# A fused attention and SiLU kernel: weight sums moved to GpSimd, one run of exponentials in chunk 2, row sums later in chunks 3 to 6

## The chip, the cores and the metric

The kernel runs on one core of a Trainium2 chip. The metric is the device time of one execution in microseconds. A profile is one such execution; its span is some 2 us shorter than the time.

## The reference, cut to what matters

```python
q_s = softmax(q, over head_dim)          # exp, row sum, divide
k_s = softmax(k, over sequence)
kv  = einsum('bhsd,bhse->bhde', k_s, v)
x   = einsum('bhsd,bhde->bhse', q_s, kv)     # 8 batches, 8 heads, 576 rows, 64
x   = x.transpose(0, 2, 1, 3).reshape(4608, 512)
h   = x @ w_in                           # 512 -> 2048
out = (h * sigmoid(h)) @ w_out           # 2048 -> 512
```

## The kernel before

The 4608 rows are worked in nine chunks, 0 to 8 (0 has 576 rows, 1 has 448, the others 512). While TensorE computes the two products of one chunk, the attention of the next batch is woven in: ScalarE takes the exponentials, VectorE the row sums (`qsum`), GpSimd the normalisation (`qnorm`) and v's cast (`vcast`, into the tile vaug), a DMA the transpose of q (`tr_dma`), TensorE the `kv` product and the product with q (`xt`), which gives the next chunk's input XT. The silu results are the tile GT; PSUM, in banks, holds what TensorE computes until another engine has read it.

From chunk 2 on both products are done with seven block products instead of eight, which needs sums of weight blocks (`vsum` for the input weights, tiles TX; `wsum` for the output weights, tiles TW) and of activations. An instruction list is built by hand: `plan(t, i, f)` puts f in front of unit i of chunk t, `ahead(t, n, f)` counts in a finer unit, `trail` puts work behind a unit. The order of the list is the order on every engine and on the DMA queue, and this is the whole of the tuning.

```python
def product1(t, g, k):                  # input product, group g of two blocks, block product k
    ...                                 # banks of PSUM: A for k = 1, 2; B for 6, 7, 4; C for 5, 3
    if k == 1:   ... new("s1") = o      # copy s, on VectorE for g = 1, else on ScalarE
    elif k == 6: add(new("u2"), s1)     # VectorE reads bank B; product 7 then adds to bank B
    elif k == 7: add(new("u3"), s1)
    elif k == 2: silu(o)
    else:        add(x, x); silu(x)     # 5, 4, 3
...
def after(t, k, o):                     # the same for the output product, trailing by one chunk
    if k == 1:
        nc.scalar.activation(out=new("s1"), in_=o, func=ACT.Copy, scale=1.0)   # "copy s" below
    elif k == 6:
        add(new("u2"), WP[t, "s1"])
    ...
ORDER = (1, 6, 2, 7, 5, 4, 3)
...
def plan_attn(b, plan, ex, qs, vs, tp, ks, ox, lq, lkv, eng=nc.gpsimd):
    for i in range(4):
        plan(ex[i], exp ...)                              # two of q, two of k
    for cc in range(2):
        plan(qs[cc], lambda cc=cc: (qsum(b, cc), qnorm(b, cc, nc.gpsimd)))
        plan(vs[cc], lambda cc=cc: vcast(b, cc, eng))
    ...
    plan(lq, lambda: load(b + 1, "qt", q))                # the next q
    plan(lkv, ...)                                        # the next k and v
    plan(tp, lambda: tr_dma(b, nc.sync))                  # transpose of q, issued from SyncE
    for cc in range(2):
        plan(ks[cc], lambda cc=cc: (kv(b, cc), kvcopy(b, cc)))
    for cc in range(2):
        plan(ox[cc], lambda cc=cc: xt(b, cc))             # reads the transposed q (qT)
```

The softmax here doesn't subtract the row's maximum and nothing guards it: scores larger than these inputs give would overflow.

## Time and profile before

| | before |
|---|---|
| time | 288.26 us, median of 4 runs (287.57 to 288.55) |
| span of the profile | 286.7 us |
| TensorE busy | 262.6 us (92%) |
| VectorE, ScalarE, GpSimd busy | 215.9, 174.0, 52.3 us |

TensorE is the bound on the whole, but not everywhere. Below I cut the span at the first matmul of the input product of each chunk, because that instruction is easy to find and the stages then add up. The first fence is the view of stretches: start and end in us, length, busy time of TensorE, its weight loads, VectorE, ScalarE and GpSimd with numbers of instructions, granted TensorE clock (the share of full speed at which TensorE was let run), DMA share and GB/s. The stretches are chunk 1, chunk 2 and two of the four steady chunks that have attention (3 to 6).

```profile
49.76:74.76 25.00, 22.55 (x189) 10.39 (x189) 20.41 (x37) 14.61 (x24) 6.43 (x4) 1.00 0.82 261
74.76:102.93 28.17, 22.66 (x206) 12.25 (x205) 19.95 (x38) 22.64 (x31) 6.85 (x4) 1.00 0.71 222
131.98:160.53 28.55, 27.04 (x301) 21.41 (x300) 23.96 (x46) 19.92 (x30) 6.39 (x4) 1.00 0.63 181
160.53:189.10 28.57, 27.06 (x302) 21.40 (x301) 23.98 (x46) 19.92 (x30) 6.39 (x4) 1.00 0.60 183
```

The reader is to see that chunk 2 has 5.5 us without TensorE work, chunk 1 2.4 us, a steady chunk 1.5 us. The view of waits (engine and line that waited, for whom, us in total, times, longest) says what these were:

```profile
PE hps L287 <- DVE u L301: 9.7, 12, 2.5
PE hps L287 <- ACT s L315: 1.4, 1, 1.4
PE ops L438 <- DVE GT L230: 1.3, 2, 1.1
PE hps L209 <- DVE GT L230: 0.6, 1, 0.6
```

L287 is the input product from chunk 2 on, L301 the VectorE sum that frees its bank. Of the 9.7 us some 3.3 lie in chunk 2 and 5.9 in the four steady chunks. There the timeline (start, length, engine, line, idle before in brackets) shows the order that the change is about:

```profile
137.88 0.68 DVE L313 TENSOR_SCALAR s<-hps 128x512 f32<-128x512 f32 x1
138.47 1.34 DVE L107 TENSOR_REDUCE zq<-eq 128x18 f32<-128x1152 bf16 x1
140.10 0.63 DVE L301 SCALAR_TENSOR_TENSOR u<-hps,s 128x512 f32<-128x512 f32 x1
140.65 1.34 DVE L107 TENSOR_REDUCE zq<-eq 128x18 f32<-128x1152 bf16 x1
140.78 0.60 PE L287 MATMUL hps<-XS,TX 128*128 128x256 bf16 x4 [1.26 <-DVE u L301]
142.57 0.62 ACT L401 ACTIVATE s<-ops 128x512 f32<-128x512 f32 x1
143.32 1.04 PE L379 MATMUL ops<-W,GT 128*128 128x256 bf16 x8
145.64 2.73 SPq L124 DMA_TRANSPOSE qT<-eq  x1
152.74 0.41 PE L189 MATMUL o<-qT,kvn 64*64 64x320 bf16 x8
```

The first row sum (L107) stands in front of the sum u, and TensorE waits 1.26 us for u. The transpose (L124) goes out 13.7 us after the chunk's first matmul (131.98), and its reader (L189) comes 7.1 us after that, so there is slack.

### The profile page before, as it was taken

How to read it: one execution, taken by the hardware profiler on the slowest of the kernel's cores; microseconds unless marked ns; L12 is line 12 of the kernel's file. 1: busy time of each engine (PE TensorE's matmuls, PEld its weight loads, DVE VectorE, ACT ScalarE, POOL GpSimd, SP SyncE). 2: the span in 40 equal slices, each digit the busy share in tenths (PEclk: the TensorE clock that was granted, in tenths of full speed). 3: DMA queues.
4: the chain of work that ended last, by engine and by line, in shares of the span. 5: the costliest groups of instructions: out<-in, count | busy, mean ns of one | idle time of the engine just before them, and what ended most of it. 6: DMA issues, size and time to landing. Idle time of an engine off the chain costs nothing.

```text
span 286.7 us, 6264 instructions
## 1 busy us (share of the span) xinstructions
PE 262.6 (92%) x2529; PEld 186.5 (65%) x2546; DVE 215.9 (75%) x422; ACT 174.0 (61%) x277; POOL 52.3 (18%) x44
## 2 busy tenths in 40 slices
PE   8789999988994988999799979997999999999993
PEld 3456664434343546876688668866876888688782
DVE  2957667897447999788978897889788769958841
ACT  5646663753799589566956695669564455454300
POOL 0541140026017004400440044004400000000000
PEclk9979999999999999999999999999999999999999
DMA  7999998985819940598069705961513011301324
GB/s 255 285 195 285 293 283 236 365 273 92 321 18 266 292 151 3 93 359 269 7 79 377 263 10 98 363 239 31 111 31 82 10 39 38 75 8 34 82 63 110
DMA packets 42381, 46.48 MB, mean 162 GB/s; under 512 B 18544, under 2 KB 29808, under 8 KB 42352
## 3 DMA queue, kind: packets, MB, share of 16 engines
q1 hardware_dynamic: 37312, 38.35, 45.1%
q0 software_dynamic: 5040, 7.73, 12.2%
q8 instruction: 20, 0.33, 0.5%
q14 instruction: 9, 0.07, 0.1%
HBM read 36.70 MB, written 9.44 MB: 161 GB/s over the span
## 4 chain that ended last, share of the span: by engine, by line
PE 60%; DVE 23%; ACT 6%; DMA 4%; issue 2%; POOL 1%; SPq 1%; DVEq 0%; POOLq 0%
PE ops L379 25%; PE hps L287 16%; PE hps L209 10%; PE ops L438 5%; DVE u L301 5%; DMA vt<-in_v_dram 3%; DVE zq L107 3%; DVE TW L355 2%; PE kvps L155 2%; PE o L189 2%; DVE SW L343 2%; DVE GT L230 2%; DVE u L396 1%; DVE SW L337 1%; ACT GT L309 1%
## 5 line engine op out<-in xcount | busy, mean ns | idle before, releaser
L209 PE MATMUL hps<-XT,W 128*128 128x512 bf16 (+3 forms) x313 | 63.6, 342 | 1.7 <-DVE GT L230 0.6
L113 POOL TENSOR_TENSOR eq<-eq,rzq 128x1152 bf16<-128x1152 bf16 x14 | 29.6, 2117 | 137.7 <-DVE rzq L108 125.5
L309 ACT ACTIVATE GT<-u 128x512 bf16<-128x512 f32 x40 | 25.2, 630 | 46.0 <-DVE u L301 46.0
L209 PEld LDWEIGHTS <-W 128*128 128x128 bf16 x320 | 31.4, 100 | 27.0 <-issue 4.0
L379 PEld LDWEIGHTS <-GT 128*128 128x128 bf16 x448 | 43.8, 98 | 7.7
L301 DVE SCALAR_TENSOR_TENSOR u<-hps,s 128x512 f32<-128x512 f32 x40 | 27.1, 678 | 22.0 <-ACT s L315 14.8
L287 PEld LDWEIGHTS <-TX 128*128 128x128 bf16 x320 | 30.3, 97 | 15.9 <-issue 11.7
L287 PE MATMUL hps<-XS,TX 128*128 128x256 bf16 x240 | 34.8, 273 | 5.0 <-DVE u L301 5.0
L379 PEld LDWEIGHTS <-SW 128*128 128x128 bf16 x336 | 32.8, 98 | 4.0 <-DVE SW L339 0.2
L230 DVE SCALAR_TENSOR_TENSOR GT<-sg,hps 128x320 bf16<-128x320 f32 (+3 forms) x64 | 23.9, 414 | 13.0 <-ACT sg L218 12.5
L438 PE MATMUL ops<-W,GT 128*128 128x512 bf16 x119 | 31.5, 380 | 1.8 <-DVE GT L230 1.3
L218 ACT ACTIVATE sg<-hps 128x320 f32<-128x320 f32 (+2 forms) x48 | 21.3, 456 | 18.6 <-PE hps L209 10.3
L379 PE MATMUL ops<-TW,SW 128*128 128x256 bf16 x224 | 28.8, 273 | 0.0
L379 PE MATMUL ops<-TW,GT 128*128 128x256 bf16 x224 | 28.7, 273 | 0.0
L379 PE MATMUL ops<-W,GT 128*128 128x256 bf16 x224 | 28.7, 273 | 0.0
L107 DVE TENSOR_REDUCE zq<-eq 128x18 f32<-128x1152 bf16 x16 | 21.5, 1344 | 9.2 <-ACT eq L93 9.2
L301 DVE SCALAR_TENSOR_TENSOR u<-hps,u 128x512 f32<-128x512 f32 x40 | 27.4, 685 | 1.0
L287 PEld LDWEIGHTS <-W 128*128 128x128 bf16 x240 | 22.5, 98 | 7.5 <-issue 4.5
L287 PE MATMUL hps<-XT,W 128*128 128x256 bf16 x160 | 24.1, 273 | 1.4 <-ACT s L315 1.4
L200 ACT CAST XT<-o 128x512 bf16<-128x512 f32 (+3 forms) x36 | 18.3, 561 | 4.5 <-PE o L189 4.5
L438 PEld LDWEIGHTS <-GT 128*128 128x128 bf16 x128 | 12.3, 98 | 13.3 <-DVE GT L230 2.3
L234 ACT ACTIVATE GT<-hps 128x512 bf16<-128x512 f32 x32 | 17.5, 595 | 3.5 <-PE hps L209 3.2
(68 smaller groups left out, 337.1 us busy)
## 6 DMA issues: line engine op xcount, KB each, us to landing
qt<-in_q_dram SPq DMA_DIRECT2D x6, 1152.0 KB, 6.2
kt<-in_k_dram SPq DMA_DIRECT2D x6, 1152.0 KB, 7.4
vt<-in_v_dram SPq DMA_DIRECT2D x6, 1152.0 KB, 9.9
W<-in_moe_w_in_dram POOLq DMA_DIRECT2D x4, 512.0 KB, 9.7
W<-in_moe_w_out_dram POOLq DMA_DIRECT2D x4, 512.0 KB, 17.4
out_dram<-oq SPq DMA_DIRECT2D x16, 128.0 KB, 6.8
out_dram<-u SPq DMA_DIRECT2D x30, 64.0 KB, 2.1
out_dram<-u SPq DMA_DIRECT2D x13, 128.0 KB, 2.4
```

The costliest lines, as they stand in the source:

```text
L107: nc.vector.reduce_sum(out=st[b]["zq"][:, cc], in_=e, axis=AX.X)
L113: eng.tensor_tensor(out=e, in0=e, in1=r[:, :, :, None].to_broadcast([128, J, 2, D]), op=ALU.mult)
L200: nc.scalar.copy(out=x, in_=o1[g][:, 0:size])
L209: nc.tensor.matmul(out=hps[:, 0:size], lhsT=W1[:, c, fb * 128:(fb + 1) * 128], rhs=XT[t][:, c, off:off + size], start=(c == 0), stop=(c == ...
L218: nc.scalar.activation(out=sg[:, 0:size], in_=hps[:, 0:size], func=ACT.Tanh, scale=0.5)
L230: nc.vector.scalar_tensor_tensor(out=y, in0=sg[:, h], scalar=1.0, in1=hps[:, h], op0=ALU.add, op1=ALU.mult)
L234: nc.scalar.activation(out=y, in_=hps[:, h], func=ACT.Silu)
L287: nc.tensor.matmul(out=o[:, f, :], lhsT=l(c, 2 * g + f), rhs=r(c), start=bool(first and f == 0 and c == 0), stop=(c == HK - 1), skip_group ...
L301: nc.vector.scalar_tensor_tensor(out=out, in0=o, scalar=1.0, in1=x, op0=ALU.mult, op1=ALU.add)
L309: nc.scalar.activation(out=y, in_=x, func=ACT.Silu)
L379: nc.tensor.matmul(out=o[:, a, :], lhsT=l(f), rhs=r(f), start=bool(first and a == 0 and f == 0), stop=(f == HF - 1), skip_group_check=True,)
L438: nc.tensor.matmul(out=OP[t, tb], lhsT=GT[t][:, fc, tb * 128:(tb + 1) * 128], rhs=W2[:, fc, :], start=(fc == 0), stop=(fc == NFB - 1),)
```

## The change

The intent: take sixteen-bit weight sums off VectorE, which is busy for 20 of 25 us in chunk 1; give chunk 2 one run of exponentials and so two table loads fewer (in this trace ScalarE loads a table, for 1.28 us, each time that it goes from silu to exponentials or back), and interleave its two groups so that each group's VectorE work hides behind the other's matmuls; and put the row sums of the steady chunks behind the sums that TensorE waits for. A copy of one element on GpSimd (`gate`) keeps its sums behind VectorE's last input-weight sum. The line `y1` also brings the output product of chunk 1, and with it its stores, forward in chunk 2. The whole diff:

```diff
@@ xlist
-        p = sorted((7 * g + POS[m], g, m) for g in range(first, HF // 2) for m in ORDER)
+        if t == STD:
+            p = [(m, g, m) for m in ORDER for g in range(first, HF // 2)]
+        else:
+            p = sorted((7 * g + POS[m], g, m) for g in range(first, HF // 2) for m in ORDER)
@@
-    y1 = [(1, x) for x in (5, 6, 8, 9, 10, 11, 13, 14, 15)] + [(2, x) for x in (1, 3, 5, 7, 10, 13, 16)]
+    y1 = [(1, x) for x in (5, 6, 8, 9, 10, 11, 13, 14, 15)] + [(2, x) for x in (0, 1, 2, 3, 4, 6, 8)]
@@
     V = nc.vector
+    G = nc.gpsimd
     for i in range(4):
-        plan(1, i, lambda i=i: vsum(i, 4, HF))
-        plan(1, 4 + i, lambda i=i: wsum(i // 2, i % 2, V))
-        plan(2, 2 * i + 10, lambda i=i: wsum(2 + i // 2, i % 2, V))
-        plan(2, 2 * i + 4, lambda i=i: vsum(i, F0, 4))
+        ahead(1, (-3, -1, 1, 2)[i], lambda i=i: vsum(i, F0, HF))
+    plan(1, 3, lambda: G.tensor_copy(gate[:, 1:2], TX[3][0:1, 0, 0:1]))
+    for i in range(8):
+        plan(1, 3 if i < 4 else 12, lambda i=i: wsum(i // 2, i % 2, G))
@@
-    plan_attn(3, lambda i, f: plan(2, i, f), (4, 4, 9, 9), (6, 8), (9, 11), 10, (14, 16), (18, 20), 7, 12)
+    plan_attn(3, lambda i, f: plan(2, i, f), (2, 2, 2, 2), (4, 6), (6, 7), 8, (12, 15), (18, 20), 7, 10)
     for b in range(4, B):
-        plan_attn(b, lambda i, f: plan(b - 1, i, f), (1, 1, 1, 1), (5, 7), (6, 7), 10, (13, 16), (19, 21), 11, 12)
+        plan_attn(b, lambda i, f: plan(b - 1, i, f), (1, 1, 1, 1), (8, 10), (6, 9), 11, (13, 16), (20, 22), 11, 12)
```

## The prediction

> **What bounds the kernel now.** TensorE is busy 262.6 of 286.7 us (page, part 1); only its gaps can be won. By stretches and waits: the stage of chunk 1 (50-75 us) has 1.9 us of TensorE waits for VectorE's GT, chunk 2 (75-103 us) 5 us (2.5 us on a VectorE sum, 1.4 us on ScalarE's copy, behind five table loads of 1.28 us), and each of the four steady chunks with attention (103-218 us, 28.56 us apart) 1.5 us on VectorE's u, behind the row sum (1.34 us + 0.27 us).
>
> **Removed, added, moved.**
> VectorE loses eight output-weight sums (8.1 us with lock waits) and gains about 0 on the input-weight sums: four of 1536 columns, some 0.97 us each (from 0.39 at 512 and 0.68 at 1024), for 5.4 us in eight. Two table loads go: 2.6 us of ScalarE.
> GpSimd gains eight sums. It needs 2.12 us for 1152 columns of the same operation, so I estimate 1.9 us each, 15 us in all. The Trainium skill (GPSIMD Engine Reference, Engine selection) says GpSimd is about 2x slower with two inputs; this trace has 2.12 against VectorE's 1.36 us.
> The Trainium skill (SBUF — State Buffer, two separate sides) says that two-input VectorE work waits out a GpSimd instruction: the trace agrees, a sum at 59.6 us took 2.40 us instead of 0.68, ending as GpSimd's ended. Here the gate keeps the input sums out of it.
>
> **Chunk 1: 0 (-0.5 to +1).** VectorE's stalls vanish, but four GpSimd sums (55.1 to about 62.8) stand before the two q normalisations, so these end near 67.1, as now (66.9). v's cast and the transpose follow; TensorE meets the cast at 68 as now. The 1.9 us gained come back as a wait for GpSimd.
>
> **Chunk 2: -4 us (-5 to -2.5).** One exponential run; pairs of groups hide the VectorE latency; VectorE loses some 6 us. Some 1.6 us remain where the PSUM ring fills during the run, perhaps 1 us at the output of the transpose, which now sits behind six stores.
>
> **Chunks 3-6: +1.4 us each (-0.1 to +2).** The row sum's wait of 1.3 us disappears, but TensorE then meets its next limit: the second product's first half must wait for ScalarE's copy s, which ends 143.19 in the chunk starting at 132 (exponentials, table load, three silus before it). That product starts at 143.32 now. So nothing is gained. Meanwhile the row sum now stands behind a VectorE sum that waits for that same copy: first sum about 138.5 -> 143.8, second 140.65 -> 146.7, transpose 145.6 -> 150.8. The transpose lands 4.7 us after issue: 155.5. The unit that reads qT now comes near 154.0: a new wait of about 1.5 us. Its slack in the kernel before was 2.4 us (150.35 against 152.74).
>
> **Sum.** 288.4 + 0.1 - 4.0 + 4 x 1.4 = about 290. Predicted 289.9 us, 8 in 10 within 284.0 to 293.0. Chances: faster by over 2% 0.05, within 2% 0.87, slower 0.08.
>
> **What would show it.** Chunk 3's start 4 us earlier; steady spacing near 30 us instead of 28.56; TensorE waits at the qT matmuls (XT outputs) for a DMA, none on VectorE's u after the row sum; GpSimd sums of 1.9 us; in chunk 1 a TensorE wait for GpSimd's vaug near 66-68 us; three table loads in chunk 2's stretch instead of five.
>
> **What would make it wrong.** If the transpose lands sooner or ScalarE reaches copy s earlier, the steady chunks are neutral and the total is about 284.5. If GpSimd sums take longer than 2.1 us, chunk 1 grows. If VectorE's later row sums also stall second-group products, steady chunks cost more.

## The result, and the profile after

| | before | after |
|---|---|---|
| time, median of 4 runs | 288.26 us (287.57 to 288.55) | 300.26 us (298.92 to 300.85) |
| ratio | | 1.0413 (95%: 1.0371 to 1.0455) |
| span of the profile | 286.7 us | 298.7 us |
| VectorE, ScalarE, GpSimd busy | 215.9, 174.0, 52.3 us | 211.0, 172.0, 69.7 us |
| chunk 1 | 25.00 us | 27.09 us |
| chunk 2 | 28.17 us | 30.55 us |
| chunks 3 to 6 | 114.73 us | 122.91 us |
| from chunk 7's first matmul to the end | 69.0 us | 69.0 us |

The four stages account for the whole loss: 2.1 + 2.4 + 8.2 us, less 0.6 us by which chunk 1 began earlier in this profile (runs with identical code up to there differ by as much: it began at 48.4 to 49.8 us in the kernel before and in runs r2 and r6 below). VectorE, ScalarE and the number of table loads all went down as intended, and the kernel became slower.

The same view of stretches after the change: chunk 1, chunk 2, and chunks 4 and 5.

```profile
49.13:76.22 27.09, 23.97 (x192) 10.98 (x188) 15.88 (x31) 14.31 (x24) 22.05 (x13) 0.94 0.80 264
76.22:106.77 30.55, 23.47 (x208) 12.88 (x205) 14.79 (x31) 20.38 (x30) 7.55 (x5) 0.89 0.62 154
138.18:168.34 30.16, 27.67 (x303) 21.60 (x300) 24.89 (x46) 20.04 (x30) 6.44 (x4) 1.00 0.53 155
168.34:199.52 31.18, 27.67 (x303) 21.58 (x300) 24.95 (x46) 20.16 (x30) 6.69 (x4) 1.00 0.66 185
```

The column before the last two is new evidence: the granted clock was 0.94 and 0.89 in the two stages where it had been 1.00. The waits:

```profile
PE o L189 <- DMA qT<-eq: 9.3, 5, 5.5
PE hps L287 <- ACT s L315: 2.9, 4, 0.7
PE kvps L155 <- POOL vaug L100: 2.8, 1, 2.8
PE ops L379 <- ACT s L401: 2.1, 4, 0.5
PE hps L287 <- DVE s L313: 1.9, 4, 0.5
PE hps L287 <- DVE u L301: 1.4, 5, 0.6
```

TensorE's waits on VectorE's u fell from 9.7 to 1.4 us, as intended. In their place stands a wait that the kernel before did not have at all, on the transposed q (first line): 5.5 us of it in chunk 2. A second new one, 2.8 us on v's cast by GpSimd, is in chunk 1. The GpSimd timeline of chunk 1 and TensorE's instruction that waited:

```profile
54.31 4.20 POOL L355 TENSOR_TENSOR TW<-W 128x1024 bf16<-128x1024 bf16 x2
58.48 4.21 POOL L355 TENSOR_TENSOR TW<-W,TW 128x1024 bf16<-128x1024 bf16 x2
62.65 4.18 POOL L113 TENSOR_TENSOR eq<-eq,rzq 128x1152 bf16<-128x1152 bf16 x2
66.79 2.24 POOL L100 CAST vaug<-vt 128x1152 bf16<-128x1152 f32 x2
67.99 0.48 PE L155 MATMUL kvps<-vaug,ek 64*64 64x65 bf16 x36 [2.76 <-POOL vaug L100]
```

Chunk 2, the DMA queue of SyncE, first before the change:

```profile
84.01 0.37 SPq L84 DMA_DIRECT2D qt<-in_q_dram  x1
87.87 1.12 SPq L457 DMA_DIRECT2D out_dram<-oq  x2
89.10 2.83 SPq L124 DMA_TRANSPOSE qT<-eq  x1
```

and after it, with the wait behind it:

```profile
88.74 3.69 SPq L457 DMA_DIRECT2D out_dram<-oq  x6
92.48 0.58 SPq L84 DMA_DIRECT2D qt<-in_q_dram  x1
93.17 5.93 SPq L124 DMA_TRANSPOSE qT<-eq  x1
102.56 0.48 PE L189 MATMUL o<-qT,kvn 64*64 64x320 bf16 x4 [5.51 <-DMA qT<-eq]
```

The transpose stands behind six stores and directly behind a load of 1.15 MB; its issue took 5.93 us instead of 2.7, and it landed 9.3 us after the issue began, where 4.7 was the median before. Last, the steady chunk that answers to the one shown before (chunk 4, which here begins at 138.18):

```profile
145.07 0.68 DVE L313 TENSOR_SCALAR s<-hps 128x512 f32<-128x512 f32 x1
145.85 0.69 DVE L301 SCALAR_TENSOR_TENSOR u<-hps,s 128x512 f32<-128x512 f32 x1
148.78 0.62 ACT L401 ACTIVATE s<-ops 128x512 f32<-128x512 f32 x1
149.43 0.69 DVE L396 SCALAR_TENSOR_TENSOR u<-ops,s 128x512 f32<-128x512 f32 x1 [1.51 <-ACT s L401]
149.45 1.03 PE L379 MATMUL ops<-W,GT 128*128 128x256 bf16 x8 [0.51 <-ACT s L401]
150.04 1.34 DVE L107 TENSOR_REDUCE zq<-eq 128x18 f32<-128x1152 bf16 x1
154.09 0.60 PE L287 MATMUL hps<-XT,W 128*128 128x256 bf16 x4 [0.73 <-ACT s L315]
157.20 2.70 SPq L124 DMA_TRANSPOSE qT<-eq  x1
161.99 0.28 PE L189 MATMUL o<-qT,kvn 64*64 64x192 bf16 x4 [0.42 <-DMA qT<-eq]
```

The sum u now comes right behind the copy of L313, but TensorE meets ScalarE's copy s (L401) instead: its output product (L379) starts 11.27 us into the chunk, against 11.34 before (143.32 less 131.98). So nothing was won there. The first row sum starts 11.9 us into the chunk instead of 6.5, the transpose goes out 19.0 us into it instead of 13.7, and the second group's product waits for ScalarE (L315) behind late VectorE sums.

The new line for batches 4 to 7 does one thing more. The first cast of v (unit 6) now stands ahead of the normalisation (unit 8) in GpSimd's list, so it runs 2.6 to 4.5 us into each of these chunks (in the kernel before 10.4 to 10.9, behind the normalisation), and one two-input VectorE sum beside it takes 1.4 us instead of 0.4. TensorE's wait of up to 0.5 us for L313 (1.9 us in all four) follows. This is not what the chunks lose: in chunk 3 of run r3 below the cast comes later and the long sum is missing, and the chunk takes 31.37 us against 31.41 in the changed kernel.

### The profile page after: what moved, and what is told of

Read it like the earlier page. It is cut to its first block, busy times and chain, and to the rows that moved or that the text cites. A ratio compares the mean times of both kernels' runs of the same rounds, so it can differ in the third digit from the quotient of the medians.

```text
span 298.7 us, 6269 instructions
## 1 busy us (share of the span) xinstructions
PE 265.3 (89%) x2546; PEld 187.6 (63%) x2546; DVE 211.0 (71%) x410; ACT 172.0 (58%) x275; POOL 69.7 (23%) x53
## 4 chain that ended last, share of the span: by engine, by line
PE 33%; DMA 19%; ACT 15%; DVE 13%; POOL 8%; issue 6%; SPq 3%; POOLq 1%; DVEq 0%; ACTq 0%
PE ops L379 15%; PE hps L287 8%; DMA W<-in_moe_w_out_dram 7%; DMA qT<-eq 7%; PE hps L209 5%; POOL eq L113 4%; PE ops L438 4%; DVE zq L107 4%; ACT ek L93 4%; ACT eq L93 3%; DVE u L301 3%; DMA kt<-in_k_dram 2%; ACT GT L234 2%; ACT L234 2%; DVE u L396 2%
## 5 line engine op out<-in xcount | busy, mean ns | idle before, releaser
L379 PEld LDWEIGHTS <-GT 128*128 128x128 bf16 x448 | 43.8, 98 | 10.4 <-issue 2.8
L301 DVE SCALAR_TENSOR_TENSOR u<-hps,s 128x512 f32<-128x512 f32 x40 | 27.2, 683 | 18.5 <-PE hps L287 8.2
L379 PEld LDWEIGHTS <-SW 128*128 128x128 bf16 x336 | 32.8, 98 | 4.0 <-DVE SW L339 0.2
L287 PE MATMUL hps<-XS,TX 128*128 128x256 bf16 x240 | 34.6, 273 | 0.8 <-DVE u L301 0.8
L287 PEld LDWEIGHTS <-TX 128*128 128x128 bf16 x320 | 30.7, 99 | 7.0 <-issue 3.0
L438 PE MATMUL ops<-W,GT 128*128 128x512 bf16 x128 | 33.7, 387 | 1.1 <-DMA W<-in_moe_w_out_dram 0.9
L218 ACT ACTIVATE sg<-hps 128x320 f32<-128x320 f32 (+2 forms) x48 | 21.3, 454 | 20.2 <-PE hps L209 14.9
L379 PE MATMUL ops<-W,GT 128*128 128x256 bf16 x224 | 28.7, 272 | 2.1 <-ACT s L401 2.1
L287 PEld LDWEIGHTS <-W 128*128 128x128 bf16 x240 | 23.1, 99 | 11.6 <-issue 8.0
L100 POOL CAST vaug<-vt 128x1152 bf16<-128x1152 f32 x12 | 14.6, 1224 | 65.7 <-DMA vt<-in_v_dram 50.3
L379 PE MATMUL ops<-TW,SW 128*128 128x256 bf16 x224 | 28.8, 273 | 0.0
L379 PE MATMUL ops<-TW,GT 128*128 128x256 bf16 x224 | 28.7, 273 | 0.0
L287 PE MATMUL hps<-XT,W 128*128 128x256 bf16 x160 | 23.9, 273 | 4.8 <-ACT s L315 2.9
```

Source lines behind the costliest of these rows:

```text
L218: nc.scalar.activation(out=sg[:, 0:size], in_=hps[:, 0:size], func=ACT.Tanh, scale=0.5)
L287: nc.tensor.matmul(out=o[:, f, :], lhsT=l(c, 2 * g + f), rhs=r(c), start=bool(first and f == 0 and c == 0), stop=(c == HK - 1), skip_group ...
L301: nc.vector.scalar_tensor_tensor(out=out, in0=o, scalar=1.0, in1=x, op0=ALU.mult, op1=ALU.add)
L379: nc.tensor.matmul(out=o[:, a, :], lhsT=l(f), rhs=r(f), start=bool(first and a == 0 and f == 0), stop=(f == HF - 1), skip_group_check=True,)
L438: nc.tensor.matmul(out=OP[t, tb], lhsT=GT[t][:, fc, tb * 128:(tb + 1) * 128], rhs=W2[:, fc, :], start=(fc == 0), stop=(fc == NFB - 1),)
```

## The experiments

Twelve kernels ran; all were correct. Stage lengths are cut as above. "Changed kernel" is the kernel after. The theories that the expectations name are these. Theory 1: the steady chunks lose because the row sums stand behind a sum that waits for ScalarE's copy s. Theory 2: chunk 2 loses by the company and place of the transpose in the DMA queue. Theory 3: chunk 1 loses by GpSimd sums in front of the normalisation. Theory 4: a long wait also costs clock. Theory 5: in the kernel before, the wait for u is in the shadow of another limit.

### The row sums of chunks 3 to 6

**r1_rows_back**, the line for batches 4 to 7 put back:

```diff
-  (1, 1, 1, 1), (8, 10), (6, 9), 11, (13, 16), (20, 22), 11, 12)
+  (1, 1, 1, 1), (5, 7), (6, 7), 10, (13, 16), (19, 21), 11, 12)
```

> The changed kernel with only the placement of the row sums, casts, transpose and output units of batches 4 to 7 put back. Theory 1 (the four steady chunks cost 8.2 us because the row sum stands behind a sum that waits for ScalarE's copy s, so that the transpose is 5 us later): steady spacing back to 28.56 us, no TensorE wait for qT there, span about 290.5 us. Rival (the steady chunks are slow because they inherit VectorE or DMA lateness from chunk 2): spacing stays 30 to 31 us and the span stays near 298 us.

Measured: chunks 4 to 6 took 28.55 us each, no wait for qT was left in chunks 3 to 6, the span was 290.5 us. The rival fell: nothing is inherited from chunk 2.

**r2_rows_only**, the same line of the change put into the kernel before:

> The kernel before with only that placement of batches 4 to 7 taken from the change. Theory 1: chunks 0 to 2 as before (chunk 3 starts near 103 us), steady spacing 30 to 31.4 us, span about 295 us. Rival (the loss needs the rest of the change): spacing 28.6 us and a span near 287 us.

Measured: chunks 1 and 2 as before (24.99 and 28.18 us), chunks 3 to 6 123.16 us in sum against 114.73, span 293.9 us. The loss of the steady chunks needs nothing of the rest of the change.

**r12_only_sums_back**: of that line only the row sums (with the normalisations that follow them) put back.

```diff
-  (1, 1, 1, 1), (8, 10), (6, 9), 11, (13, 16), (20, 22), 11, 12)
+  (1, 1, 1, 1), (5, 7), (6, 9), 11, (13, 16), (20, 22), 11, 12)
```

> The changed kernel with only the row sums and normalisations of batches 4 to 7 put back to their two units; casts, transpose and output units stay where the change put them. If the place of the row sums is what costs the steady chunks: the transpose goes out 14 us after a chunk's first matmul as in the kernel before (19 in the changed one), no wait for qT in chunks 3 to 6, the wait of 1.3 us for u is back, spacing 28.4 to 28.7 us, span about 290.5. Rival (the later transpose, output units or cast cost it too): spacing over 29.2 us.

Measured: chunks 4 to 6 took 28.56 to 28.57 us; the transpose went out 14.0 us into chunk 4; the wait of 1.3 us for u was back and none for qT in these chunks; span 291.1 us. So it is the place of the row sums, not the units given to the casts, the transpose or its readers. (The first cast comes 10 to 11 us into the chunk again, behind the normalisation, though its unit is the change's.)

**r9_copy_dve**: is it ScalarE's copy s that makes them late, as theory 1 has it?

```diff
-        if k == 1:
+        if k == 1 and 2 <= t <= 5:
+            nc.vector.tensor_scalar_mul(out=new("s1"), in0=o, scalar1=1.0)
+        elif k == 1:
             nc.scalar.activation(out=new("s1"), in_=o, func=ACT.Copy, scale=1.0)
```

> The changed kernel with the copy s of the output product taken from ScalarE to VectorE in chunks 3 to 6 only (one more VectorE instruction of 0.68 us a chunk, one less on ScalarE). Theory 1 says that the row sums are late because the VectorE sum in front of them waits for ScalarE's copy behind the exponentials: then the first row sum starts 2 to 3 us earlier in the chunk, the transpose goes out about 2.5 us earlier (16.5 us after the chunk's first matmul instead of 19), no TensorE wait for qT over 0.3 us is left, nor one for copy s, and the spacing falls from 30.2 to 31.4 us to between 27.5 and 28.8. Rival (the sheer place of the row sums among VectorE's work makes them late, whoever copies s): the transpose moves by under 1 us and the spacing stays over 29.8 us.

Measured: the row sum of chunk 4 came 11.1 us into the chunk instead of 11.9, the transpose 18.3 instead of 19.0, and the chunk took 29.39 us instead of 30.16; the four took 119.6 us instead of 122.9. A wait for qT was left (8.9 us in all five chunks, 5.4 of it in chunk 2), and TensorE now waited up to 1.1 us for VectorE's own copy (L313), which stands behind the added one. The spacing lies between theory and rival. The 0.8 us is what is left of the copy's share after two things that this edit puts in front of the row sum: the added copy itself (0.7 us), and the sum held up beside the cast, which in the changed kernel is hidden behind the wait for copy s (1.51 us, shown above) and here is not. In chunk 3 of r11, which has the same later row sums and copy but no such hold-up, the row sum comes 10.0 us into the chunk, against 12.0 in chunk 3 of the changed kernel and 7.0 before. So ScalarE's copy is some 0.8 to 1.9 us net of the delay of about 5 us, and theory 1 holds in part: the rest is the place in VectorE's list, behind a sum that needs matmuls which only end 10 us into the chunk.

**r6_rows_sooner**: the kernel before with the first row sum one unit later only.

```diff
-  (1, 1, 1, 1), (5, 7), (6, 7), 10, (13, 16), (19, 21), 11, 12)
+  (1, 1, 1, 1), (6, 7), (6, 7), 10, (13, 16), (19, 21), 11, 12)
```

> The kernel before with the first row sum of batches 4 to 7 issued one unit later only, that is just behind the first product's sum u that TensorE waits 1.3 us for, and ahead of the sum that needs copy s. Theory 5 (that wait is in the shadow of ScalarE's copy s, behind the exponentials, so taking it away gains nothing): the wait for u falls from 1.3 us to under 0.3 us a chunk, a wait for copy s of about 1.4 us appears in its place, the spacing stays 28.5 us (within 0.15) and the span 286 to 287.5. Rival (the wait was worth its length, and the change only moved the row sums too far): spacing 27.2 us and a span near 281.

Measured: spacing 28.76 us (0.2 us longer than before, just outside what I had expected), span 287.0. The rival fell. But the wait did not pass to copy s as I had expected: both row sums now stand together in front of the next sum, and TensorE waits 1.8 us for that one. The run shows that the wait for u cannot be had back by this step; it doesn't show by itself that copy s is the limit.

### Chunk 2 and the transpose

**r3_load_behind**: in the line of batch 3, the load of the next q behind the transpose.

```diff
-  (2, 2, 2, 2), (4, 6), (6, 7), 8, (12, 15), (18, 20), 7, 10)
+  (2, 2, 2, 2), (4, 6), (6, 7), 8, (12, 15), (18, 20), 9, 10)
```

> The changed kernel with one line moved in chunk 2: the load of the next q (1.15 MB) is issued behind the transpose of batch 3 instead of just ahead of it. Theory 2 (the transpose landed 9.3 us after issue instead of 4.7 because it shares the DMA engines with that load): the transpose is still issued near 92.5 us, lands in 4.7 us near 97.3, TensorE's wait for qT in chunk 2 falls from 5.5 to about 0.5 us, and chunk 3 starts 5 to 6 us earlier. Rival (the transpose is only late because it stands behind six stores in the queue): landing stays 9 us and the wait stays over 4 us.

Measured: the transpose was issued at 91.11 us, in 2.82 us, and TensorE's wait ended at 97.48, 6.4 us after the issue instead of 9.4; the wait fell from 5.5 to 1.9 us and chunk 2 from 30.55 to 26.72 us. The company of the load is most of it. Some of the wait stays, more than expected, because the transpose still took 6.3 us to land and not 4.7.

**r7_tr_early**: also the transpose in front of the last four stores of chunk 1.

```diff
-  (2, 2, 2, 2), (4, 6), (6, 7), 8, (12, 15), (18, 20), 7, 10)
+  (2, 2, 2, 2), (4, 6), (6, 7), 6, (12, 15), (18, 20), 9, 10)
```

> The changed kernel with, in chunk 2, the transpose of batch 3 issued ahead of the last four of the eight output stores of chunk 1, and the load of the next q behind it. Theory 2 (place in the queue and company of the load together make the 5.5 us wait): the transpose goes out near 90 us, as soon as its input is normalised, TensorE's wait for qT in chunk 2 is under 0.7 us, chunk 2 lasts 25 to 26 us instead of 30.5, 2 to 3 us less than in the kernel before. Rival (something else holds chunk 2 back, as the PSUM ring or the exponentials): it stays above 27 us.

Measured: the transpose landed 4.8 us after its issue, there was no wait for qT in chunk 2, and the chunk took 24.53 us, 3.6 us less than in the kernel before. The queue of SyncE, to be held against the one shown above:

```profile
88.38 2.41 SPq L457 DMA_DIRECT2D out_dram<-oq  x4
90.89 2.81 SPq L124 DMA_TRANSPOSE qT<-eq  x1
93.80 2.48 SPq L457 DMA_DIRECT2D out_dram<-oq  x4
96.33 1.05 SPq L84 DMA_DIRECT2D qt<-in_q_dram  x1
```

The Trainium skill (DMA: Bandwidth & Descriptors, Queues, rings and completion order) says that one issuing engine's descriptors are consumed in ring order on each DMA engine. The three runs agree with it: the transpose landed 9.3 us after its issue with the load in front of it (changed kernel), and 6.3 and 4.8 us with the load behind it (r3 and r7). A run with the place alone mended, the load still in front, was not made.

### Chunk 1 and GpSimd

**r4_sums_late**: the GpSimd sums behind the normalisations.

```diff
-        plan(1, 3 if i < 4 else 12, lambda i=i: wsum(i // 2, i % 2, G))
+        plan(1, 12, ...wsum(i // 2, i % 2, G)) if i < 4 else plan(2, 9, ...wsum(i // 2, i % 2, G))
```

> The changed kernel with the eight GpSimd sums moved behind the q normalisations: four behind v's casts in chunk 1, four in chunk 2. Theory 3 (in chunk 1 TensorE waits 2.8 us for v's cast because four GpSimd sums of 2.1 us stand in front of it, and the granted clock of 0.62 in the 4 us after that wait costs another 1.5 us): no wait for vaug, granted clock 1.00 between 64 and 72 us, chunk 2 starts near 72 us instead of 76.2. Rival (what delays the cast is the late row sums on VectorE, not GpSimd's own work): the wait stays at 2 us or more.

Measured: no wait for v's cast, granted clock 1.00 from 60 to 76 us, chunk 1 22.71 us: 4.4 less than in the changed kernel and 2.3 less than before. Chunk 2 began at 71.4 us. In the GpSimd timeline the normalisations now come as soon as the row sums are there:

```profile
57.30 2.12 POOL L113 TENSOR_TENSOR eq<-eq,rzq 128x1152 bf16<-128x1152 bf16 x1 [3.37 <-ACT sg L218]
59.87 2.12 POOL L113 TENSOR_TENSOR eq<-eq,rzq 128x1152 bf16<-128x1152 bf16 x1 [0.46 <-ACT sg L218]
61.93 2.26 POOL L100 CAST vaug<-vt 128x1152 bf16<-128x1152 f32 x2
64.14 4.21 POOL L355 TENSOR_TENSOR TW<-W 128x1024 bf16<-128x1024 bf16 x2
```

The rival, late row sums, falls: in the changed kernel they were there some 5 us before their normalisation began.

### What a wait costs besides its length

**r5_fill_wait**: the changed kernel with idle matmuls in the two long waits.

```diff
+    def fill(n):
+        w = ps.tile([128, 512], FP32, name="fill", tag="ring", bufs=PSB["ring"])
+        for _ in range(n):
+            nc.tensor.matmul(out=w, lhsT=warm[:, 0:128], rhs=warm, start=True, stop=True)
+    plan(1, 13, lambda: fill(11))
+    plan(2, 18, lambda: fill(23))
```

> The changed kernel with idle matmuls (128x128 by 512, on zeros, result unread) put where TensorE waits: 11 in front of the first kv matmuls of batch 2 in chunk 1, 23 in front of the first qT matmuls of batch 3 in chunk 2. Theory 4 (after a wait the granted clock is about 0.5 for some microseconds, so a wait costs more than its own length): the two waits end when they end in the changed kernel (v's cast near 68, the transpose near 102.5), but the granted clock stays 1.00 after them; from the first qT matmuls waited for to chunk 3's first matmul takes about 2.9 us instead of 4.2, and chunk 3 starts 1.3 to 2.7 us earlier. Rival (the slower matmuls behind the waits come from their own stalls, as on PSUM buffers): the intervals stay as in the changed kernel.

Measured, with the view of stretches, first the changed kernel and then this run (from 68 to 72 us, and from 102.5 to 106.8 us):

```profile
68.00:72.00 4.00, 4.00 (x81) 1.97 (x81) 1.44 (x6) 0.54 (x1) 4.00 (x3) 0.62 1.01 179
102.50:106.80 4.30, 4.24 (x29) 2.46 (x29) 2.76 (x5) 2.54 (x5) 0.00 (x0) 0.54 0.98 307
```

```profile
68.00:72.00 4.00, 3.95 (x87) 2.14 (x87) 2.24 (x9) 0.98 (x2) 4.00 (x3) 1.00 0.98 172
102.50:106.80 4.30, 3.50 (x24) 1.77 (x20) 3.73 (x7) 3.71 (x7) 0.00 (x0) 1.00 1.02 386
```

The cast came at 68 us in both, but chunk 1 took 25.52 us instead of 27.09. From the first qT matmuls waited for to chunk 3's first matmul it took 2.71 us (100.88 to 103.59) instead of 4.21 (102.56 to 106.77). Chunk 3 began 3.2 us earlier, somewhat more than expected. The clock is thus about 1.5 us at each of the two waits. For chunk 2 the other profiles bear this out: the clock was low behind the unfilled wait of 5.3 to 5.5 us in all five that have it (changed kernel, r1, r4, r9, r12). The whole run gained nothing (298.9 us of span), because in chunks 4 and 5 the transposes happened to take 6.3 and 6.6 us to land, the waits for qT were 2.0 and 2.2 us, the clock fell to 0.82 (190 to 195 us) behind the second, and these chunks took 31.7 and 33.5 us; this I have not tested.

The Trainium skill (TensorE: Matmul & The Clock Gate, Part 1) says that a monitor of TensorE's activity halves its clock after an idle window of some 3.4 us that runs freely, so that the moment varies from run to run. The runs agree with the variation: the same wait of 2.8 us for the cast was followed by a clock of 0.62, 0.58, 0.67 and 0.60 (from 68 to 72 us) in the changed kernel, r1, r7 and r12, where chunk 1 took 26.8 to 27.2 us, and of 1.00 in r3 and r9, where it took 25.5 us. So the full clock in chunk 1 of r5 could by itself be chance; that the slow clock costs 1.2 to 1.6 us there is shown by all of these together.

### All mends together

**r8_all_mended**: the edits of r1, r7 and r4 in one kernel.

> The three mends together: GpSimd sums behind the normalisations, the transpose early and the load behind it in chunk 2, batches 4 to 7 placed as in the kernel before. If the three causes account for the whole loss: chunk 1 22.7 us, chunk 2 25 to 26, steady spacing 28.55, span 280 to 282 us, about 282.5 us against 288.3 (ratio 0.98). If they overlap or a fourth cause is left, the span stays above 284 us.

Measured in three rounds: 284.06 us (283.19 to 284.15) against 289.43 for the kernel before on the same chip (287.65 to 289.69), ratio 0.9825 (95%: 0.9799 to 0.985). Chunk 1 took 22.71 us, chunk 2 26.23, chunks 4 to 6 28.55 to 28.56, span 281.2. The three causes account for the loss, and this version beats both kernels, the kernel before by 1.75%, which is clear of the noise (whether it is 2% is not). Two things differ from what I expected. Chunk 2 is 1.7 us longer than in r7: TensorE waits 1.0 us more there, for a VectorE sum, and the granted clock is 0.60 from 96 to 100 us, over the start of chunk 3, which took 29.7 us (29.05 before). And 1.95 of the 5.5 us by which the span is shorter than before are an earlier start of chunk 1 (47.8 us).

**r10_mended_copy_dve** (r8 with the edit of r9) and **r11_mended_newrows_copy** (r8 with the change's later row sums and the edit of r9) asked whether the steady chunks can be had below 28.5 us by moving one limit or both.

> The mended kernel (batches 4 to 7 as before, GpSimd sums late, transpose early) with the same copy on VectorE. In the kernel before TensorE's wait for u behind the row sum ends just as ScalarE's copy s comes, so two limits stand in one place. Theory 5: with only the copy moved, the row sum's limit stays and VectorE gets 0.7 us more to do in front of it: spacing 28.4 to 29.2 us, span 281 to 283 us. Rival (the copy alone was the limit): spacing 27.5 us or less, span under 277.5.

Measured: 29.15 us a chunk (4 to 6), 287.29 us, ratio 0.9946 (0.9906 to 0.9986). The spacing is as expected; the span, 286.0, is not, since in this profile chunk 1 began at 50.3 us instead of 47.8 and chunk 3 took 30.2.

> The mended chunks 1 and 2, the change's later row sums, and the copy on VectorE: both limits of the steady chunks moved at once. Theory 5: now the spacing falls under that of the kernel before, to 27.2 to 28.3 us, span 276 to 280.5 us, about 280 us in time (ratio 0.97). Rival (a third limit stands right behind, as the transpose or the copies of the second group on ScalarE): spacing 28.5 us or more.

Measured: 29.0 to 30.3 us a chunk (4 to 6), 289.80 us, ratio 1.0025 (0.998 to 1.007), with waits of up to 2.0 us for qT. The rival was right: with both limits moved, VectorE's own copy and the transpose are there at once. I found no version of the steady chunks below 28.5 us; that those of the kernel before are balanced between VectorE, ScalarE and the transpose is my reading of these runs and not shown by one of them.

## Why the prediction was wrong

The prediction was 289.9 us, within 284.0 to 293.0; it is 300.26. Of the 10.4 us in between chunk 2 holds 6.4, chunks 3 to 6 hold 2.6 and chunk 1 holds 2.0, less the 0.6 us by which chunk 1 began earlier. By stages, against the kernel before:

| stage | predicted | measured | what the difference is |
|---|---|---|---|
| chunk 1 | 0 (-0.5 to +1) | +2.1 us | the clock after the wait, about 1.5 us (r5); the cast 0.5 us later in the chunk |
| chunk 2 | -4 (-5 to -2.5) | +2.4 us | wait for qT 5.5 us instead of 1 (r3, r7), clock 1.5 us (r5) |
| chunks 3 to 6 | +1.4 each (-0.1 to +2) | +2.0 each on average | later second-group sums; landing 5.8 to 5.9 us in two of the four |

**Chunk 1: the wait was right, its cost was not.** I had written that four GpSimd sums would end near 62.8 us and the normalisations near 67.1, and that TensorE would meet the cast at 68. They ended at 62.7 and 66.8, and TensorE went on at 68.0. The size of a GpSimd sum was off (1.9 predicted, 2.11 measured) and made up for by an earlier start. The failing step is "The 1.9 us gained come back as a wait for GpSimd": I counted the wait as its own length. It came back with a slower clock: the chunk took 26.8 to 27.2 us in the four profiles with a low clock behind this wait, and about 25.5 us in the two with full clock and in r5. The remaining 0.5 us is the cast: since chunk 1 began earlier in this profile, 68.0 us is 18.9 us into the chunk, against 18.3 before.

**Chunk 2: the step that failed is "perhaps 1 us at the output of the transpose, which now sits behind six stores".** I had seen the stores. I had not counted that the load of the next q also goes out just in front of the transpose, because it stands behind the same stores; before, that load was issued at 84.0 us and the transpose at 89.1. The wait was 5.5 us, and some 1.5 us of slow clock came behind it. With load and place mended the wait is gone, and the chunk takes 3.6 us less than before (r7). That this is near the -4 us is in part luck: 1 us of wait for the transpose was counted in the -4, so the rest, one exponential run and pairs of groups, was put 1.4 us too high. In r7 TensorE waits 1.3 us for ScalarE's cast of the first XT output instead. The ring wait of 1.6 us was measured as 1.3. No run separates what the single exponential run and the pairs of groups gave.

**Chunks 3 to 6: the direction was right; the step that failed is "The transpose lands 4.7 us after issue".** No gain from the removed wait, a limit at copy s in the same place (11.27 against 11.34 us into the chunk), the first row sum 11.9 us into the chunk (11.8 predicted), the transpose 5 us later, a new wait for qT: all this is in the trace, and r1, r2 and r12 tie it to the place of the row sums. The landing was 4.8 us in chunks 4 and 6, which lost 1.6 us each against the kernel before, near the 1.4 predicted. It was 5.8 to 5.9 us in chunks 3 and 5, where TensorE waited 1.6 and 1.4 us for qT, and these lost 2.4 and 2.6 us. The 1.6 us itself came about otherwise than predicted, which is luck: in chunk 4 the wait for qT is 0.4 us and not 1.5, because TensorE is 1.0 us late already at its second group's second product (L287 at 15.9 us into the chunk, 14.9 before), which I had named as a risk and not added. The reason given for the late row sum, a VectorE sum that waits for copy s, is in the trace but is the smaller part of it (r9, r11). Why the landing varies I have not settled; it took 6.1 us in chunk 4 of the kernel before too, where the slack hid it.

The range was too narrow for a plan in which three stages each depended on a DMA or a wait of a size never seen in the profile before.

## What to carry to other kernels

Before moving work to an idle engine, list what stands behind it in that engine's queue: GpSimd was idle by the busy table, yet the normalisation behind it was on the way to TensorE. The same holds for a DMA queue: one transfer moved behind some stores also came to stand behind a large load, and that cost more than the stores. And when a wait of some microseconds on TensorE is predicted, add to it the slower clock that can follow.

## What the Trainium skill lacked or had wrong

- TensorE: Matmul & The Clock Gate (Why this matters for your kernels) advises against idle gaps above some 3 us. Here a gap of 2.8 us was enough in four of six profiles (granted clock 0.58 to 0.67 in the 4 us from 68), at a cost of 1.2 to 1.6 us. Shorter gaps were followed by half the clock for 3.4 us too: 2.2 us in r5 (from 193.2 us), 2.0 us in r11 (from 122.9 us), and two of 1.3 and 1.0 us 0.3 us apart in r8 (from 95.8 us); a wait of 2.5 us in chunk 2 of the kernel before was not. Behind the 5.5 us of chunk 2 it was half for 6.8 us (from 99.6 us in the changed kernel).
- GPSIMD Engine Reference (Engine selection) gives GpSimd as about 2x slower for two-input work. For a bf16 subtraction of 128x1024 it is 3.1 times: 2.11 us against 0.68 us on VectorE. The page's factor also doesn't tell that the 1152-column product takes no longer (2.12 us) than the 1024-column difference.
- SBUF — State Buffer (Who interferes with whom) lacked nothing here and was confirmed: a VectorE sum with two inputs in SBUF took 1.40 us instead of 0.42 while a GpSimd cast ran (141.27 us in the profile after).
- No page that I read gives the time to landing of a transpose from SBUF to SBUF in company: 4.7 us was the median for 128x2304 elements in the kernel before, and 9.3 us in the changed one with a 1.15 MB load directly in front of it in the same queue; without such a load it still took up to 6.6 us (r5, chunk 5).
